# A planner that lays out a fused attention and gated-layer kernel: the first instruction of a tile becomes a condition of order alone for its other users

## Chip, cores and metric

One Trainium2 chip, one core of it. The kernel is written in Bass and Tile: it names the instructions of the engines itself, and the Tile layer adds the semaphores. The metric is the device time of one execution in microseconds (us). TensorE is called PE, VectorE DVE, ScalarE ACT, GpSimd POOL, and SyncE, whose queue issues most transfers, SP.

## The reference

A local attention (chunks of 32 queries, up to 64 keys with 8 of memory, 4 x 8 heads, 768 tokens, head dimension 64) feeds two gated layers on 3072 tokens with 512 features.

```python
scores = scale * np.matmul(q_c, k_full.transpose(0, 1, 3, 2))
a = np.exp(scores - max); a = a / (sum + 1e-9); out = a @ v_full
...
gate = 1.0 / (1.0 + np.exp(-(x @ w_gate)))          # 512 -> 1536
x = (gate * (x @ w_val)) @ w_out                     # 1536 -> 512
...
h = x @ w_in                                         # 512 -> 2048
P = a[0] + a[1]*h + a[2]*h**2 + a[3]*h**3
Q = 1.0 + abs(b[0])*abs(h) + abs(b[1])*h**2
y = (P / (Q + 1e-06)) @ w_out2                       # 2048 -> 512
```

Inputs and result are float32; the weights come as 64-bit words and are turned into float32 on the chip.

## The kernel before

**Work.** Every float32 operand of a large matrix product is split into a high part (an ACT copy to the reduced format) and the rest (a DVE subtraction), and three products of parts replace one. The tokens are cut into six blocks of 512 (index j). In the first layer, for block j and feature group f (12 of them), PE makes `h{j}_{f}_0` (gate) and `h{j}_{f}_1` (value), 12 matmuls of 512 columns each; ACT takes the sigmoid of the first into a tile called `sg{j}_{f}` (or, where two tiles share a buffer, by the name of the other half, as `wfo2` or `wfo7`); DVE multiplies; ACT and DVE split the product into `g1_{j}_{f}`; and 12 matmuls add it to `acc{j}`. The weights of group f come in three loads, `st1_{f}_0` to `st1_{f}_2`. For f = 1 and 2 the three loads share two buffers: `stp1_0` holds 1_1_0 and 1_1_1, `stp1_1` holds 1_1_2, and `stp2_0`, `stp2_1` likewise. `conv_scale` makes two ACT operations of 512 columns on each load, `conv_bits` one DVE operation that merges them (into `wfgv` or `wfo`), and then `wp1_{j}_{f}_{u}` is split off it, high part on ACT, rest on DVE.

**Start.** The attention of the first four groups of 128 tokens stands at the head of the program. For group t: `sp` (scores, PE), maximum, exponential and sums (DVE, ACT), a DVE multiplication `s<-s,r`, `tp` (four transposes, PE), an ACT copy `at<-tp`, `xp` (64 short products, PE), and the split of `x` (ACT copy `x<-xp`, DVE rest). Filler matmuls (`idle<-ones`) stand between them on PE. Then the first layer begins with `h0_0_0`.

**What sets the order.** Nothing is issued directly. A `Recorder` notes every call as a `Task` with the tiles that it touches. Its `plan()` runs the tasks through a model with costs of its own and hands out, engine by engine, the ready task with the earliest due time (`late`); `emit()` then issues them in that order. PE's order is fixed as written, so the planner only sets the order of ACT, DVE, POOL and SP around it. A task becomes a candidate when all tasks in its `deps` have been placed (`missing` is 0), and not before the time at which their results are there (`ready`). Due times run backwards over the same dependencies. In `access()` the first task that touches a tile of a pool (`c.first`) takes the buffer, and each other user of that tile gets it as a dependency:

```python
elif c.first is not t:
    t.deps.add(c.first)
```

So the second transfer into a half of `stp1_0` waited in the plan for the landing of the first, though the two halves are apart. Dependencies through the data itself are found further down in the same function, by overlapping regions. Buffers of PSUM are the `ps` pool (4 banks, shared by `sp`, `tp`, `xp` and `h`) and `acc`.

On the chip each engine works through its list in order and waits at the head for semaphores. All calls go through line 471 in the trace (line 480 with the change); tiles tell them apart.

Of the kernel before, what the change touches and what calls it, by code (L numbers as in the profile page):

```python
# [53 lines left out]
class Cell:  # L54


    def __init__(self, pool, make, dt, real=None):
        self.pool, self.make, self.dt, self.real = pool, make, dt, real
        self.accesses, self.users, self.first, self.group, self.left = [], set(), None, None, 0
# [115 lines left out]
class Task:  # L175
    def __init__(self, eng):
        self.eng, self.calls, self.deps, self.cells, self.gets = eng, [], set(), set(), []
        self.dur, self.lat, self.bytes, self.start, self.table, self.mark = 0.0, 0.15, 0, None, None, None
        self.window, self.cap, self.soon, self.late, self.fixed = 30.0, None, 0.0, 0.0, False
        self.ordered = True  # L180
# [10 lines left out]
class Recorder:  # L191
# [77 lines left out]
    def access(self, t, x, write):  # L269
        c, box = x.cell, x.box()  # L270
        if c.pool is not None and t not in c.users:
            if c.first is None:
                c.first = t
                t.gets.append(c)
            elif c.first is not t:
                t.deps.add(c.first)
            c.users.add(t)
            t.cells.add(c)
        keep = []
        for b, u, w in c.accesses:  # L280
            if b[0] < box[1] and box[0] < b[1] and b[2] < box[3] and box[2] < b[3]:
                if u is not t and (write or w):
                    t.deps.add(u)
                inside = box[0] <= b[0] and b[1] <= box[1] and box[2] <= b[2] and b[3] <= box[3]
                if write and inside or u is t and w == write and inside:
                    continue
            keep.append((b, u, w))
        keep.append((box, t, write))
        c.accesses = keep
# [24 lines left out]
    def plan(self):  # L314
        tasks = self.tasks
        for t in tasks:
            t.succ = []
        for t in tasks:
            t.missing, t.soft = len(t.deps), []
            for d in t.deps:  # L320
                d.succ.append(t)
            t.ready = 0.0
# [6 lines left out]
        for t in reversed(tasks):  # L329
            t.succ, t.hard = t.succ + t.soft, t.succ  # L330
            if t.eng == "tensor":
                t.late = min([t.soon] + [u.late - t.lat * (u.eng != "tensor") - t.dur for u in t.succ])
                continue
            lat = t.lat + (4.5 if t.bytes else 0)
            cap = t.cap if t.cap is not None else self.DMA_CAP if t.bytes else self.CAP
            t.late = min([t.soon + cap] + [u.late - lat - t.dur for u in t.succ])
        free = dict(self.sizes)
        cells = {c for t in tasks for c in t.cells}
        for c in cells:
# [14 lines left out]
        ready = {e: [t for t in tasks if t.eng == e and not t.missing] for e in engines}  # L354
        busy, dma, table = dict.fromkeys(engines, 0.0), 0.0, None
        order, ends, half, now, stall, left = [], [], None, 0.0, 0.0, len(tasks)
        events = []
        self.stalls = []
        while left:
            while ends and ends[0][0] <= now + 1e-9:  # L360
                free[heapq.heappop(ends)[1]] += 1
            moved = False
            for e in engines:
                if busy[e] > now + 1e-9:
                    continue
                head = fixed.get(e)
                if e == "tensor":
                    pick = pe[pe_i : pe_i + 1]
                elif head:
                    pick = head[:1]  # L370
                else:
                    pick = ready[e]
                best = None
                for t in pick:
                    if t.missing or t.ready > now + 1e-9 or best and best.late <= t.late:
                        continue
                    if not t.fixed and e != "tensor":
                        if t.late > now - stall + t.window:
                            continue
                        if t.bytes and dma > now + 7 and t.late > now - stall + 9:  # L380
                            continue
                    need, h = {}, half
                    for c in t.gets:
                        if c.pool == ("t", "half"):
                            if h:
                                h = None
                                continue
                            h = True
                        need[c.pool] = need.get(c.pool, 0) + 1
                    if all(  # L390
                        free[self.real_pool(p)] >= n + 2 * (n == 3) + (0 if t.fixed or p[0] not in (self.ORDERED if t.ordered else "g") else bisect_left(waiting[p], t.key))
                        for p, n in need.items()
                    ):
                        best = t
                if best is None:
                    continue
                t = best
                if e == "tensor":
                    pe_i += 1
                    if now - t.soon > stall + 0.05:  # L400
                        self.stalls.append((now, now - t.soon - stall, t))
                    stall = max(stall, now - t.soon)
                elif head:
                    head.pop(0)
                if e != "tensor":
                    ready[e].remove(t)
                extra = 0.0
                if t.table and t.table != table:
                    table, extra = t.table, 1.29
                t.start = now  # L410
                busy[e] = now + t.dur + extra
                end = now + t.dur + extra + t.lat
                if t.bytes:
                    dma = max(dma, now + 0.8) + t.bytes / self.RATE
                    end = dma + t.lat
                for c in t.gets:
                    waiting[c.pool].remove(t.key)
                    if c.pool == ("t", "half"):
                        if half:
                            c.group, half = half, None  # L420
                            c.group[0] = 2
                            continue
                        half = c.group = [1, 0, 0.0]
                    else:
                        c.group = [1, 0, 0.0]
                    free[self.real_pool(c.pool)] -= 1
                for c in t.cells:
                    c.left -= 1
                    g = c.group
                    g[2] = max(g[2], end)  # L430
                    if c.left == 0:
                        g[1] += 1
                        if g[1] == 2 or g[1] == g[0] and g is not half:
                            heapq.heappush(ends, (g[2], self.real_pool(c.pool)))
                for u in t.hard:
                    u.missing -= 1
                    u.ready = max(u.ready, end if u.eng != e or e != "tensor" else now + t.dur)
                    if not u.missing and u.eng != "tensor":
                        ready[u.eng].append(u)
                    heapq.heappush(events, u.ready)  # L440
                heapq.heappush(events, busy[e])
                order.append(t)
                left -= 1
                moved = True
            if not moved:
                while events and events[0] <= now + 1e-9:
                    heapq.heappop(events)
                nxt = events[0] if events else None
                if ends and (nxt is None or ends[0][0] < nxt):
                    nxt = ends[0][0]  # L450
                for e in engines[1:]:
                    for t in ready[e]:
                        w = t.late + stall - t.window
                        if now + 1e-9 < w and (nxt is None or w < nxt):
                            nxt = w
                if dma > now + 7:
                    nxt = dma - 7 + 1e-3 if nxt is None else min(nxt, dma - 7 + 1e-3)
                assert nxt is not None, (now, free, left, pe[pe_i].calls[0], [(e, len(ready[e])) for e in engines])
                now = max(nxt, now + 1e-6)
# [1606 lines left out]
```

## Time and profile before

| | us |
|---|---|
| median of 3 runs (lowest, highest) | 1134.45 (1133.39, 1134.48) |
| the profiled execution | 1134.46 |
| its span, first to last instruction | 1132.6 |
| PE busy | 1120.2 |
| DVE busy | 872.8 |
| ACT busy | 750.1 |

The 1.86 us between the profiled execution's time and its span lie outside the instructions. A busy PE is not PE at its peak, since matmuls are pipelined and their modelled ends overlap; what counts below are the times at which PE waits, and from one matmul's start to the next (2.72 us for 12 of 512 columns).

### The profile page before, as it was taken

To read this page: it belongs to the slowest core of one execution; us is meant where nothing else is said; L and a number is where in the kernel's file an instruction comes from. 1 tells how busy PE (TensorE), PEld (TensorE's weight loads), DVE (VectorE), ACT (ScalarE), POOL (GpSimd) and SP (SyncE) were. 2 spreads that over 40 slices of the span, in tenths; PEclk is the share of its full clock that TensorE was granted. 3 is DMA by queue.
4 is the path that set the end of the run, shared out by engine and by line. 5 is a ranking of instruction groups with operands and counts; after the bars stand their busy time and mean duration, and the time that the engine had idled before them with its cause. 6 is when DMAs were issued, how large, how long until landed. Compare 5 with 4: busy or idle time off the path is not lost.

```text
span 1132.6 us, 20033 instructions
## 1 busy us (share of the span) xinstructions
PE 1120.2 (99%) x7815; PEld 918.5 (81%) x7815; DVE 872.8 (77%) x1184; ACT 750.1 (66%) x1105; POOL 23.1 (2%) x39
## 2 busy tenths in 40 slices
PE   8999999999999999999999999999999999999998
PEld 4787888888888888888888788888888888888887
DVE  5788867774676667565568499999899999789984
ACT  4999556663454466343345599875799974898852
POOL 0000000000000000000000000000000000000000
PEclk8999999999999999999999999999999999999999
DMA  9899699997978799898976576689677788576764
GB/s 371 311 352 360 227 347 363 350 365 259 379 279 324 288 376 387 310 373 291 322 259 246 191 230 220 208 246 342 203 229 225 223 288 307 167 242 219 230 207 143
DMA packets 100318, 318.78 MB, mean 281 GB/s; under 512 B 10752, under 2 KB 11008, under 8 KB 100224
## 3 DMA queue, kind: packets, MB, share of 16 engines
q1 hardware_dynamic: 96192, 303.51, 74.3%
q0 software_dynamic: 3456, 12.58, 6.0%
q8 instruction: 62, 1.02, 0.4%
q10 hardware_dynamic: 576, 1.41, 0.3%
q14 instruction: 32, 0.26, 0.1%
HBM read 240.91 MB, written 63.96 MB: 269 GB/s over the span
## 4 chain that ended last, share of the span: by engine, by line
PE 96%; ACT 1%; DMA 1%; DVE 1%; issue 0%; DVEq 0%
PE acc L471 40%; PE p L471 20%; PE q_X L471 12%; PE h L471 10%; PE q_Z L471 6%; PE q_Y L471 3%; PE xp L471 2%; PE sp L471 1%; PE tp L471 1%; PE idle L471 1%; DMA st<-w_in 0%; DMA k<-k_in 0%; ACT L471 0%; ACT stp L471 0%; DVE s L471 0%
## 5 line engine op out<-in xcount | busy, mean ns | idle before, releaser
L471 PE MATMUL acc<-w2o,G 128*128 128x512 f32 x1152 | 268.4, 389 | 0.0
L471 PEld LDWEIGHTS acc<-w2o,G 128*128 128x128 f32 x1152 | 216.2, 188 | 44.9
L471 PE MATMUL acc<-g,wp 128*128 128x512 f32 x720 | 177.0, 393 | 0.0
L471 PEld LDWEIGHTS acc<-g,wp 128*128 128x128 f32 x720 | 133.3, 188 | 28.3 <-issue 0.2
L471 PE MATMUL q_X<-x,wi 128*128 128x512 f32 x576 | 146.5, 390 | 1.4 <-ACT hb L471 1.4
L471 PE MATMUL h<-x,wp 128*128 128x512 f32 x576 | 138.1, 392 | 1.7 <-ACT sg L471 0.9
L471 PE MATMUL p<-b,wpq_s 128*128 128x512 f32 x576 | 138.4, 389 | 0.0
L471 PEld LDWEIGHTS q_X<-x,wi 128*128 128x128 f32 x576 | 107.9, 188 | 24.7 <-ACT hb L471 2.5
L471 PEld LDWEIGHTS h<-x,wp 128*128 128x128 f32 x576 | 107.2, 188 | 25.0 <-ACT wp L471 1.1
L471 PEld LDWEIGHTS p<-b,wpq_s 128*128 128x128 f32 x576 | 108.1, 188 | 22.5
L471 ACT ACTIVATE st<-st 128x512 f32<-128x512 f32 (+1 forms) x124 | 76.7, 666 | 0.0
L471 PE MATMUL p<-x,wpq_a 128*128 128x512 f32 x288 | 73.2, 389 | 0.0
L471 PE MATMUL q_Z<-x,wi 128*128 128x512 f32 x288 | 73.1, 389 | 0.0
L471 ACT ACTIVATE u<-q,qc 128x1024 f32<-128x1024 f32 x48 | 54.9, 1147 | 14.4 <-DMA q<-u 13.2
L471 PEld LDWEIGHTS p<-x,wpq_a 128*128 128x128 f32 x288 | 54.0, 188 | 11.3
L471 PEld LDWEIGHTS q_Z<-x,wi 128*128 128x128 f32 x288 | 54.1, 188 | 11.2
L471 DVE SCALAR_TENSOR_TENSOR t<-t,cf,u 128x1024 f32<-128x1024 f32 x48 | 61.2, 1278 | 0.0
L471 DVE SCALAR_TENSOR_TENSOR q<-q,u 128x1024 f32<-128x1024 f32 x48 | 58.3, 1219 | 2.2 <-ACT u L471 2.1
L471 ACT ACTIVATE hb<-q_X 128x512 f32<-128x512 f32 x48 | 28.4, 592 | 36.4 <-PE q_X L471 36.3
L471 ACT ACTIVATE u<-u 128x1024 f32<-128x1024 f32 x48 | 50.3, 1055 | 0.4
L471 ACT ACT_TABLE_LOAD x31 | 39.8, 1283 | 15.8 <-PE h L471 7.2
L471 ACT ACTIVATE g<-c 128x512 fp32r<-128x512 f32 x22 | 13.8, 629 | 51.1 <-DVE c L471 51.1
(271 smaller groups left out, 1708.8 us busy)
## 6 DMA issues: line engine op xcount, KB each, us to landing
w2o<-w2o SPq DMA_DIRECT2D x96, 512.0 KB, 4.4
wi<-wq SPq DMA_DIRECT2D x72, 512.0 KB, 4.6
st<-w_in SPq DMA_DIRECT2D x62, 512.0 KB, 7.0
wp<-wqa SPq DMA_DIRECT2D x55, 512.0 KB, 6.6
wpq_s<-wqs SPq DMA_DIRECT2D x48, 512.0 KB, 8.1
wpq_a<-wqa SPq DMA_DIRECT2D x36, 512.0 KB, 7.6
wqa<-wp SPq DMA_DIRECT2D x30, 512.0 KB, 7.5
v<-v_in SPq DMA_DIRECT2D x24, 512.0 KB, 6.4
```

What stands on the lines that cost most here:

```text
L471: getattr(getattr(self.nc, t.eng), op)(*[real(x) for x in args], **{n: real(x) for n, x in kw.items()})
```

## The change

A new set `after` stands beside `deps`. The first task of a tile goes there for the other users of it, unless it is a true dependency as well. In the plan such a user may not be placed before the first task has been placed (it still counts in `missing`), but from then on it may go at once: its `ready` time is the moment of placing, not the end of the first task's work. In the due times the first task need only be as early as its user, with no duration or latency taken off.

```diff
 class Task:
     def __init__(self, eng):
         self.eng, self.calls, self.deps, self.cells, self.gets = eng, [], set(), set(), []
+        self.after = set()
...
             elif c.first is not t:
-                t.deps.add(c.first)
+                t.after.add(c.first)
...
         for t in tasks:
-            t.succ = []
+            t.succ, t.next = [], []
         for t in tasks:
-            t.missing, t.soft = len(t.deps), []
+            t.after -= t.deps
+            t.missing, t.soft = len(t.deps) + len(t.after), []
+            for d in t.after:
+                d.next.append(t)
...
-                t.late = min([t.soon] + [u.late - t.lat * (u.eng != "tensor") - t.dur for u in t.succ])
+                t.late = min([t.soon] + [u.late for u in t.next] + [u.late - t.lat * (u.eng != "tensor") - t.dur for u in t.succ])
...
-            t.late = min([t.soon + cap] + [u.late - lat - t.dur for u in t.succ])
+            t.late = min([t.soon + cap] + [u.late for u in t.next] + [u.late - lat - t.dur for u in t.succ])
...
+                for u in t.next:
+                    u.missing -= 1
+                    u.ready = max(u.ready, now)
+                    if not u.missing and u.eng != "tensor":
+                        ready[u.eng].append(u)
```

PE's list stays as it was. On SP the loads of the first weights change places; on ACT and DVE rows move mainly within blocks 0 and 1, and a few later. Three places follow. At the start, DVE's list before, from the multiplication of group 2 on (`s2<-s2,r2`; `r3` belongs to group 3, `x0_0` and `x0_1` are the first x tiles):

```order
L471 TENSOR_TENSOR s2_290<-s2_290,r2_343 128x512
L471 RECIPROCAL r3_355<-r3_355 128x8
L471 SCALAR_TENSOR_TENSOR wfgv0_410<-st1_0_0_135 128x512
L471 TENSOR_TENSOR s2_290<-s2_290,r3_355 128x512
L471 TENSOR_TENSOR x0_0_403<-xp0_0_363,x0_0_403 128x2x128
L471 TENSOR_TENSOR x0_1_412<-xp0_1_365,x0_1_412 128x2x128
L471 TENSOR_TENSOR wp1_0_0_0_418<-wfgv0_410,wp1_0_0_0_418 128x512
L471 SCALAR_TENSOR_TENSOR wfgv0_410<-stp1_0_133 128x512
```

The same stretch of DVE's list with the change:

```order
L480 SCALAR_TENSOR_TENSOR wfgv0_400<-st1_0_0_133 128x512
L480 TENSOR_TENSOR s2_292<-s2_292,r2_345 128x512
L480 RECIPROCAL r3_356<-r3_356 128x8
L480 TENSOR_TENSOR x0_0_402<-xp0_0_363,x0_0_402 128x2x128
L480 TENSOR_TENSOR s2_292<-s2_292,r3_356 128x512
L480 TENSOR_TENSOR x0_1_404<-xp0_1_365,x0_1_404 128x2x128
L480 TENSOR_TENSOR wp1_0_0_0_407<-wfgv0_400,wp1_0_0_0_407 128x512
L480 SCALAR_TENSOR_TENSOR wfgv0_400<-st1_0_1_139 128x512
```

The merge of the first weights now stands ahead of the two multiplications, and the multiplication of group 3 (by `r3`) now stands behind `x0_0`, which reads the products of group 0.

ACT's list before, from the conversion of the first weights to the table load for the first sigmoid, without the rows that read `xp` (those stand between):

```order
L471 ACTIVATE st1_0_0_135<-st1_0_0_135 128x512
L471 ACTIVATE stp1_0_133<-stp1_0_133 128x512
L471 ACTIVATE st1_0_0_135<-st1_0_0_135 128x512
L471 ACTIVATE at0_348<-tp1_357 128x512
...
L471 ACTIVATE stp2_1_231<-stp2_1_231 128x512
L471 ACTIVATE stp1_0_133<-stp1_0_133 128x512
L471 ACTIVATE stp2_0_139<-stp2_0_139 128x512
L471 ACT_TABLE_LOAD
L471 ACTIVATE wfo2_618<-h0_0_0_580 128x512
L471 ACTIVATE wp1_0_1_1_640<-wfgv0_410 128x512
```

The same two pieces of ACT's list with the change:

```order
L480 ACTIVATE st1_0_0_133<-st1_0_0_133 128x512
L480 ACTIVATE at0_349<-tp1_358 128x512
L480 ACTIVATE x0_0_402<-xp0_0_363 128x2x128
...
L480 ACTIVATE wp1_0_1_0_571<-wfgv0_400 128x512
L480 ACTIVATE st1_0_2_183<-st1_0_2_183 128x512
L480 ACTIVATE wp1_0_1_1_588<-wfgv0_400 128x512
...
L480 ACTIVATE stp2_0_230<-stp2_0_230 128x512
L480 ACT_TABLE_LOAD
L480 ACTIVATE sg0_0_627<-h0_0_0_580 128x512
```

Ahead of the copy of `tp1` one conversion operation is left of three, and `wp1_0_1_1`, the second weight tile of group f = 1, now stands eight rows ahead of the table load instead of two behind it.

The third place is on ACT around the sigmoid of `h0_7_0`, before:

```order
L471 ACTIVATE s6_1131<-s6_1131 128x512
L471 ACTIVATE wp1_0_9_0_1311<-wfgv4_1140 128x512
L471 ACTIVATE wp1_0_9_1_1349<-wfgv4_1140 128x512
L471 ACT_TABLE_LOAD
L471 ACTIVATE sg0_7_1356<-h0_7_0_1287 128x512
```

and with the change:

```order
L480 ACTIVATE s6_1127<-s6_1127 128x512
L480 ACT_TABLE_LOAD
L480 ACTIVATE sg0_7_1350<-h0_7_0_1283 128x512
L480 ACTIVATE x1_0_1357<-xp4_0_1310 128x2x128
L480 ACTIVATE x1_1_1366<-xp4_1_1312 128x2x128
L480 ACTIVATE sg0_7_1350<-tp5_1345 128x512
L480 ACTIVATE wp1_0_9_0_1371<-wfgv4_1154 128x512
L480 ACTIVATE wp1_0_9_1_1379<-wfgv4_1154 128x512
```

The two weight splits for f = 9 moved behind the sigmoid of f = 7; nothing else ahead of that sigmoid was added or taken away, only moved.

## Rows read from the trace of the kernel before

**Rows 1.** The page, part 1: busy us (share) xinstructions of each engine.

```profile
PE 1120.2 (99%) x7815; PEld 918.5 (81%) x7815; DVE 872.8 (77%) x1184; ACT 750.1 (66%) x1105; POOL 23.1 (2%) x39
```

**Rows 2.** Waits of PE, whole span: waiter, releaser, us in total, times, longest.

```profile
PE tp L471 <- DVE s L471: 3.1, 2, 1.6
...
PE q_X L471 <- ACT hb L471: 1.4, 2, 0.7
PE h L471 <- ACT sg L471: 0.9, 1, 0.9
PE h L471 <- ACT wp L471: 0.7, 1, 0.7
```

**Rows 3.** Windows: us, busy (x) of PE, PEld, DVE, ACT, POOL; clock, DMA.

```profile
40.00:95.00 55.00, 54.98 (x543) 44.31 (x542) 46.55 (x83) 54.83 (x95) 0.34 (x2) 1.00 0.94 340
125.00:260.00 135.00, 135.00 (x1518) 111.77 (x1511) 94.70 (x149) 82.26 (x138) 0.34 (x2) 1.00 0.94 344
```

**Rows 4.** Timeline of PE, 18 to 45 us: start, us, operation, count, idle before.

```profile
18.09 1.09 PE L471 MATMUL tp<-ident,s 128*128 128x128 f32 x4 [1.54 <-DVE s L471]
19.11 1.93 PE L471 MATMUL xp<-at,v 64*64 64x32 f32 x64
20.97 1.97 PE L471 MATMUL tp<-ident,s 128*128 128x128 f32 x8
22.73 1.49 PE L471 MATMUL idle<-ones 128*128 128x512 bf16 x3
24.14 1.24 PE L471 MATMUL xp<-at,v 64*64 64x32 f32 x64
...
26.07 1.14 PE L471 MATMUL xp<-at,v 64*64 64x32 f32 x64
...
27.89 1.14 PE L471 MATMUL xp<-at,v 64*64 64x32 f32 x64
...
29.86 7.19 PE L471 MATMUL h<-x,wp 128*128 128x512 f32 x30
37.76 4.73 PE L471 MATMUL h<-x,wp 128*128 128x512 f32 x18 [0.71 <-ACT wp L471]
42.33 2.88 PE L471 MATMUL acc<-g,wp 128*128 128x512 f32 x12
```

**Rows 5.** Timeline of DVE, 17 to 22 us.

```profile
17.25 0.69 DVE L471 TENSOR_TENSOR s<-s,r 128x512 f32<-128x512 f32 x1
...
20.08 0.68 DVE L471 TENSOR_TENSOR s<-s,r 128x512 f32<-128x512 f32 x1
21.50 0.76 DVE L471 TENSOR_TENSOR x<-xp,x 128x256 fp32r<-128x256 f32 x2 [0.74 <-ACT x L471]
```

**Rows 6.** Timeline of ACT, 19 to 37 us.

```profile
19.35 0.57 ACT L471 ACTIVATE at<-tp 128x512 f32<-128x512 f32 x1
21.09 0.66 ACT L471 ACTIVATE x<-xp 128x256 fp32r<-128x256 f32 x2 [1.17 <-PE xp L471]
...
31.78 3.50 ACT L471 ACTIVATE stp<-stp 128x512 int32<-128x512 uint32 x6
35.30 1.28 ACT L471 ACT_TABLE_LOAD   x1
```

**Rows 7.** Timeline of ACT, 92 to 97 us.

```profile
92.77 1.13 ACT L471 ACTIVATE wp<-wfgv 128x512 fp32r<-128x512 f32 x2
93.92 1.28 ACT L471 ACT_TABLE_LOAD   x1
95.21 0.60 ACT L471 ACTIVATE sg<-h 128x512 f32<-128x512 f32 x1
```

**Rows 8.** Timeline of PE, 92 to 97 us.

```profile
95.86 1.43 PE L471 MATMUL h<-x,wp 128*128 128x512 f32 x5 [0.88 <-ACT sg L471]
```

**Rows 9.** Windows of the start, columns as in rows 3; the clock stands before DMA.

```profile
18.00:24.00 6.00, 5.91 (x79) 4.52 (x79) 4.26 (x11) 4.46 (x10) 0.00 (x0) 0.50 1.03 404
...
26.00:30.00 4.00, 4.00 (x138) 2.84 (x137) 3.08 (x7) 3.91 (x10) 0.00 (x0) 1.00 1.02 407
```

## Prediction

> **What bounds the kernel now.** I read the page first: PE is busy for 1120.2 of 1132.6 us [rows 1], and its list is the same with the change. So time can be won only where PE waits for another engine, and lost only where a new wait arises. The list of PE's waits comes next [rows 2]. Apart from the first transfers there are four: 3.1 us for the softmax multiplication `s` on DVE (two waits, ahead of the transposes), 0.7 us for a weight split `wp` on ACT, 0.9 us for a sigmoid `sg` on ACT, and 1.4 us for `hb` copies in the second layer, where neither ACT's nor DVE's nor SP's list changes. The windows say who is short where [rows 3]: from 40 to 95 us ACT is busy for 54.83 of 55.00 us, so everything that ACT does late at the start is still late at 95 us. From 125 to 260 us it is busy for only 82.26 of 135; there and later PE has no wait until `hb`, and the few rows that move there move by one or two places. I take the change to be decided in the first 96 us.
>
> **The change part by part.**
>
> *Group 3's transposes come later.* Before, DVE multiplies group 3 at 20.08 [rows 5] and PE runs the transposes of groups 2 and 3 in one piece, 20.97 to 22.94 [rows 4], group 3's from about the middle, 21.9. With the change that multiplication stands behind `x0_0`, which can't start before 21.50, since it waits for ACT's copy of `xp0`, and PE's `xp0` is not moved by the change. Two x rows in 0.76 us with a duration of about 0.4 give a step of 0.34, so the multiplication runs from 21.85 and ends 0.69 later, at 22.54. From the end of the other `s<-s,r` (17.25 + 0.69) to the transposes that waited for it (18.09) is 0.15: PE starts at 22.69, **0.8 us later**. Fillers, `xp1` to `xp3` and the first `h` follow without a wait before, so all of them move by as much: `h` from 29.86 to 30.7.
>
> *The weights of group f = 1 come earlier.* The first 30 `h` matmuls run from 29.86; at 0.227 each (2.72 for 12) the 48 up to `acc` would take 10.9 us, to 40.75. `acc` starts at 42.33, 1.6 later. About 0.2 of that is at the very start, for the first x parts, and stays. The rest, **1.36**, is the wait for `wp1_0_1_1` at 37.76 (0.71 of it idle, the remainder the pipeline's own and the wait for the tile's DVE half). In the new list this tile's ACT half stands eight rows ahead of the table load (8 x 0.56, so before 32 us) and its DVE half follows; PE needs it at 37.7. The wait goes. `acc` then starts at 42.33 + 0.82 - 1.36 = **41.8, 0.54 earlier**.
>
> *ACT falls behind.* This is the term that I think decides. One conversion costs a step of 0.56 (six in 3.50 us, the last one 0.68) [rows 6], a weight split 0.52 (1.13 for two, 0.1 of it a tail) [rows 7], a pair of x copies 0.55 (0.66 with its tail) and a copy `at` 0.5 (0.57 with its tail) [rows 6]. Before, ACT fills the time up to the copy of `tp1` with three conversions; in the new list one is left, and the two that went don't come until PE has been waited for. I follow the new list: the copy of `tp1` at 19.22 (the transposes end at 18.09 + 1.09), `xp0` at 21.09 as before; x pair, split, conversion, `at2`, two conversions, `at3`, split, done at 25.36; `xp1` ends at 24.14 + 1.24 + 0.82 = 26.20; x pair, two conversions, 27.93; `xp2` ends at 28.03; x pair, one conversion, 29.18; `xp3` ends at 29.85; then x pair, three splits and seven conversions (0.55 + 1.56 + 3.92, and 0.16 for the last one's tail), and the table load starts at 36.1 instead of 35.30 [rows 6], 0.8 later, with one conversion fewer done. **ACT is 0.8 + 0.56 = 1.36 us behind** with everything that follows.
>
> *The sigmoid of f = 7 comes earlier in ACT's list.* Between 40 and 95 us ACT has nothing to catch up with. The sigmoid that PE waits for at 95.86 [rows 8] ends at 95.81 [rows 7]. The two splits that moved behind it take 2 x 0.52 off: 95.81 - 1.04 + 1.36 = 96.13, and PE starts at 96.18, **0.33 later than before**. PE itself would be there at 95.86 - 0.88 - 0.54 = 94.4, so 1.75 us of new waits between 42 and 95 us would be free. What PE wins at 37.76 it gives back here.
>
> *The rest at nothing.* The loads keep their number, and the first of the weights takes the same place in SP's list, with another tile. Table loads keep their number as well. The splits for f = 9 are needed at about 110 us and now come some 2 us later than before; ACT has a gap after 115 us to end its backlog in. If that cover were gone, each would cost 0.52.
>
> *Sum.* Against the profiled execution (1134.46 us, 0.01 over the median of the three runs): +0.33, so **1134.8 us**. The bounds: if the sigmoid does not hold PE up at all, -1.42 (0.88 + 0.54); if the 0.82 of the transposes is doubled for ACT by a slower start, +1.2.
>
> **Rivals.** *1. The clock stays low for longer.* [...] PE had been working without a wait since 18.09 when it rose. The new wait of some 0.6 us lies inside that stretch. It came back between 24 and 26, some 6.7 us after 18.09. If it comes back as long after 22.69, at 29.4, `xp1`, a filler and most of `xp2` run at the low level. `xp` takes 1.93 there against 1.14 [rows 4], 1.7 times; over the 2.7 us of work in question this is +1.7, and ACT passes it on in full, since it waits for each `xp`: 1136.5. If the clock stays low until `h`, the 4.9 us from `xp1` to the end of `xp3` become 8.1: +3.3, so 1138.1, and **slower**. The point from which it is slower by over 0.2% (2.27 us, about what a measurement of this kernel tells from no change) is a clock that comes back later than about 30 us. For it: the fall came after waits like this one. Against: the new wait is less than half as long as each of the two that brought the clock down, and fillers follow it. [...]
>
> *2. ACT is not behind at 95 us.* If DVE's new order lets ACT's work come so that the idle steps are made up, or the sigmoid is early for another reason, PE passes at up to 94.4 instead of 95.86: 1133.0 to 1134.2. For it: two more splits are out of the way, and PE is early. Against: ACT has no idle time to give from 40 to 95 us [rows 3].
>
> *3. Little moves.* The change reorders mainly blocks 0 and 1, and what is won and lost may cancel to 1134.5 without the gate deciding; this can't be told from my forecast by the time, only by the rows.
>
> *4. A new wait elsewhere* after 96 us, from a row that lost its place on ACT or DVE (the x combinations near 230 and 430 us, the splits near 690). Each such place would cost about one operation, 0.5 to 0.7 us; it would take four of them for 0.2%.
>
> **How the numbers follow.** My forecast (1134.2 to 1135.6): 0.63. Rival 1: 0.18 with the clock back by 30 us (up to 1136.8), 0.07 later than that. Rival 2: 0.07. Rival 4: 0.05, of which 0.02 beyond 0.2%. The likeliest time is 1134.8; from 1133.2 to 1136.7 holds some 0.85 to 0.9, the forecast, most of rival 2 and the first half of rival 1. No case that I can price wins more than 1.42 us, less than 0.2%, so faster gets 0.03, for what I have not seen; slower gets 0.07 and 0.02 and a little for the unseen, 0.10; the rest, 0.87, is within 0.2%.
>
> **What would show it.** Right: a wait of PE for `s` ahead of the second set of four transposes, near 22.1 to 22.7; `h` from about 30.7; no wait for `wp` near 38; `acc` near 41.8; the first table load of the sigmoid on ACT near 36.1; and a wait of PE for `sg` near 96, some 1.7 us long instead of 0.88, ended at about 96.2. Wrong: that wait gone or shorter than 0.9 (ACT was not behind), windows with a clock of 0.50 beyond 26 us, or a PE wait of over 0.5 us at a place that isn't named here. It goes wrong most easily through the clock, or through ACT waiting for DVE somewhere between 40 and 95 us, where each microsecond is one of the kernel.

## The result, and the profile after

The changed kernel takes 1142.31 us (median of six executions), the kernel before 1134.30 (six beside them): a ratio of 1.0057, with a 95% interval of 1.0033 to 1.0080. It is slower by 0.57%. The six lie in two groups: 1136.72 and 1137.15, and four from 1142.21 to 1142.54. The prediction was 1134.8, with a range that ended at 1136.7.

The profiled execution is the fastest one, of 1136.72 us (span 1134.7). Its list of PE's waits answers to [rows 2]:

```profile
PE tp L480 <- DVE s L480: 3.7, 3, 1.6
PE h L480 <- ACT sg L480: 1.9, 1, 1.9
```

There is a third wait for `s`, the wait for `sg` is twice as long, and the one for `wp` is gone. The timeline of PE, beside [rows 4] and [rows 8]:

```profile
20.92 1.11 PE L480 MATMUL tp<-ident,s 128*128 128x128 f32 x4
22.62 1.09 PE L480 MATMUL tp<-ident,s 128*128 128x128 f32 x4 [0.59 <-DVE s L480]
23.50 1.34 PE L480 MATMUL idle<-ones 128*128 128x512 bf16 x3
24.77 1.14 PE L480 MATMUL xp<-at,v 64*64 64x32 f32 x64
...
30.38 11.28 PE L480 MATMUL h<-x,wp 128*128 128x512 f32 x48
41.49 2.88 PE L480 MATMUL acc<-g,wp 128*128 128x512 f32 x12
...
96.06 4.60 PE L480 MATMUL h<-x,wp 128*128 128x512 f32 x12 [1.91 <-ACT sg L480]
100.50 2.88 PE L480 MATMUL acc<-g,wp 128*128 128x512 f32 x12
```

The timeline of ACT, beside [rows 6, 7]:

```profile
35.78 1.28 ACT L480 ACT_TABLE_LOAD   x1
...
95.41 0.60 ACT L480 ACTIVATE sg<-h 128x512 f32<-128x512 f32 x1
```

Every row that was forecast stands within 0.4 us of its place, and the wait at the gate of f = 7 ends at 96.06 for a forecast of 96.18. But behind that wait 12 matmuls take 4.60 us from first to last. In the kernel before, the same rows are:

```profile
95.86 3.02 PE L471 MATMUL h<-x,wp 128*128 128x512 f32 x12 [0.88 <-ACT sg L471]
98.72 2.88 PE L471 MATMUL acc<-g,wp 128*128 128x512 f32 x12
```

The windows of the changed kernel say why (the clock stands before the DMA share, as in [rows 9]):

```profile
18.00:24.00 6.00, 5.37 (x78) 4.29 (x79) 4.14 (x11) 3.85 (x9) 0.00 (x0) 0.50 1.03 404
24.00:26.00 2.00, 2.00 (x68) 1.22 (x67) 1.14 (x2) 1.40 (x4) 0.00 (x0) 0.86 0.99 391
...
95.00:100.00 5.00, 3.94 (x10) 3.12 (x11) 2.97 (x7) 4.99 (x11) 0.00 (x0) 0.66 1.03 398
```

After the wait of 1.91 us, PE's clock was at 0.50 of full speed from 97 to 99 us (0.62 in the microsecond before, 0.67 in the one after); the mean of 95 to 100 us is 0.66. In the kernel before it is 1.00 there. So in this execution PE is 0.20 us late when it leaves the wait (96.06 for 95.86), and 1.8 us late at the next `acc` (100.50 for 98.72 before). This explains most of the lower group. The upper group needed a trace of its own, which two later executions of the same kernel gave (1142.61 and 1141.76 us). Timeline of PE in the first of these:

```profile
22.77 1.09 PE L480 MATMUL tp<-ident,s 128*128 128x128 f32 x4 [0.59 <-DVE s L480]
23.65 1.49 PE L480 MATMUL idle<-ones 128*128 128x512 bf16 x3
25.07 1.93 PE L480 MATMUL xp<-at,v 64*64 64x32 f32 x64
...
35.21 11.10 PE L480 MATMUL h<-x,wp 128*128 128x512 f32 x42
...
102.08 4.60 PE L480 MATMUL h<-x,wp 128*128 128x512 f32 x12 [1.92 <-ACT sg L480]
106.52 2.90 PE L480 MATMUL acc<-g,wp 128*128 128x512 f32 x12
```

and its windows:

```profile
24.00:26.00 2.00, 2.00 (x39) 1.09 (x40) 1.12 (x2) 1.52 (x3) 0.00 (x0) 0.50 1.00 397
26.00:30.00 4.00, 4.00 (x107) 2.83 (x101) 1.69 (x4) 1.77 (x4) 0.00 (x0) 0.50 1.02 407
30.00:38.00 8.00, 8.00 (x91) 5.06 (x87) 4.19 (x8) 5.64 (x13) 0.00 (x0) 0.52 0.59 230
38.00:50.00 12.00, 12.00 (x55) 9.91 (x53) 8.19 (x14) 11.65 (x21) 0.00 (x0) 1.00 0.70 233
```

The matmuls and these two waits are the same (0.59 at 22.77, 1.92 at 102.08). But the clock stays at 0.50 from 18 to 30 us, and the mean of 30 to 38 is 0.52, where the execution of 1136.72 has it back before 26 (0.86 in 24 to 26, 1.00 in 26 to 30). The first `h` starts at 35.21 for 30.38, and the gate of f = 7 is passed at 102.08 for 96.06: 6.0 us, about what lies between the groups. Of the nine executions of the changed kernel, six are of the upper group; the 75 of the kernel before that were timed beside all runs lie between 1133.39 and 1135.57.

### The profile page after: what moved, and what is told of

It reads as the page before. It is cut to its first block, busy times and chain, and to the rows that moved or that the text cites. A ratio compares the mean times of both kernels' runs of the same rounds, so it can differ in the third digit from the quotient of the medians.

```text
span 1134.7 us, 20035 instructions
## 1 busy us (share of the span) xinstructions
PE 1121.4 (99%) x7815; PEld 919.6 (81%) x7815; DVE 873.4 (77%) x1184; ACT 751.3 (66%) x1105; POOL 23.1 (2%) x39
## 3 DMA queue, kind: packets, MB, share of 16 engines
q8 instruction: 62, 1.02, 0.3%
q10 hardware_dynamic: 576, 1.41, 0.3%
## 4 chain that ended last, share of the span: by engine, by line
PE 91%; ACT 2%; issue 0%; DVE 0%
PE acc L480 39%; PE p L480 20%; PE q_X L480 12%; PE h L480 8%; PE q_Z L480 6%; PE q_Y L480 3%; PE xp L480 2%; PE sp L480 1%; PE tp L480 1%; ACT st L480 1%; ACT wp L480 0%; ACT L480 0%; ACT hb L480 0%; ACT s L480 0%; ACT g L480 0%
```

## The experiments

Three theories stood after the first profile. **1:** the wait at 96 us brings the clock down, for a longer or a shorter time, and this makes both groups. **2:** the new wait of 0.6 us at the start (group 3's transposes) keeps the clock down for longer, in some executions. **3:** the second loss lies behind 125 us. In the edits, `order` is the list that the planner returns, just before it is issued; `at(engine, written, read)` finds a task in it, and `move(task, ahead_of)` changes its place.

**The changed kernel once more**, for the place of the second loss.

> The changed kernel as it is, for another profile: six executions gave 1136.7, 1137.2 and four times 1142.2 to 1142.5. [...] Theory 2 (the new wait of 0.6 us ahead of group 3's transposes holds the clock down at the start): a profile of about 1142 shows a clock of 0.50 beyond 25 us, h later than 31, and ACT later by as much. [...] If it comes out at 1137 again, it shows the same two shifts as before, +0.2 at 96.06 and +1.6 by 100 us.

1137.5 us, so of the lower group, with the same two waits, and so nothing new of the upper group. It has one wait more: 0.76 us for "issue" (nothing that the profile shows) among the `xp` products at 28.25. The mean clock of the whole execution is 0.995, as in the one of 1136.72, so no long stretch at 0.50 came with this wait, and the first `h` starts 1.07 us later than in the execution of 1136.72 (31.45 for 30.38). The executions of one group thus differ at the start as well.

**The wait at 96 us filled.** PE makes group 5's transposes six times instead of once, and works while the sigmoid is on its way.

```diff
+        order[at("tensor", "tp5")].calls *= 6
```

> The changed kernel, where PE makes the four transposes of tp5, the last work ahead of the wait for the sigmoid of f = 7, six times instead of once (same result each time), so that PE works through most of its 1.9 us of waiting. The order on all engines stays. Theory 1: the clock stays at full speed at 96 us, h0_7_1 starts at 96.1 as before, and the 1.6 us lost behind it and whatever makes 1142 are gone: 1135.1 (1134.7 to 1135.4) in all executions. Theory 2 or 3: the executions still fall into about 1137 and about 1142.

1137.75, 1142.44, 1142.50 and 1142.56 us. The profiled one is of the upper group. Its PE timeline and windows:

```profile
99.17 2.84 PE L503 MATMUL tp<-ident,s 128*128 128x128 f32 x24
101.76 3.00 PE L503 MATMUL h<-x,wp 128*128 128x512 f32 x12
104.59 2.88 PE L503 MATMUL acc<-g,wp 128*128 128x512 f32 x12
...
441.63 0.32 PE L503 MATMUL xp<-at,v 64*64 64x32 f32 x8 [2.02 <-issue]
```

```profile
30.00:38.00 8.00, 7.35 (x78) 5.08 (x81) 4.38 (x9) 5.92 (x13) 0.00 (x0) 0.54 0.57 222
...
95.00:100.00 5.00, 5.00 (x86) 4.14 (x86) 4.42 (x9) 4.95 (x9) 0.00 (x0) 1.00 0.97 301
```

No wait for `sg` is left, the clock doesn't fall there (1.00 in 97 to 105 us), and the 12 `h` take 3.00 instead of 4.60 us. The upper group stays all the same, with the low clock up to 38 us. Theory 1 as the cause of two groups falls, and theory 3 has its answer too: the clock is low up to 38 us here as in the execution of 1142.61 (0.54 in 30 to 38 us, for 0.52), where that had cost 6.0 us by the gate. By the next `acc` this execution is 1.93 us ahead of that one (104.59 for 106.52), 1.6 of it by the filling and 0.3 from ahead of the gate. It was lost again at 441 us, in a wait of 2.02 us for "issue" (see the end).

**The wait at 95 us of the kernel before made longer.** A weight split of ACT ahead of the sigmoid is made three times.

```diff
+        order[at("scalar", "wp1_0_9_1")].calls *= 3
```

> The kernel before, with the ACT split of wp1_0_9_1, which stands ahead of the sigmoid of f = 7, made three times instead of once (same result), 2 x 0.52 more of ACT's work: the wait at 95.86 grows from 0.88 to 1.9 us. Nothing else of the change is in it. Theory 1: 1.04 for the wait, and 1.6 for the clock that falls then: 1137.0 (1136.7 to 1137.4), with some executions near 1142. Theory 2 or 3: 1135.4, the wait alone.

Median 1135.67 (ratio 1.0018, 1.0008 to 1.0027). Of ten executions seven lie from 1135.22 to 1135.80, the others at 1137.13, 1138.75 and 1138.88. The last one is profiled:

```profile
97.45 5.49 PE L494 MATMUL h<-x,wp 128*128 128x512 f32 x12 [2.23 <-ACT sg L494]
```

```profile
97.00:105.00 8.00, 7.55 (x20) 5.96 (x21) 3.04 (x7) 6.00 (x13) 0.00 (x0) 0.58 0.79 278
```

With a wait of 2.23 us, 1.35 longer than in [rows 8], the clock falls (0.58 in 97 to 105 us), and 12 matmuls take 5.49 us. This execution also has a wait of 1.41 us for "issue" at 26.65, with a second low stretch behind it (28.8 to 32 us; the mean is 0.82 in 26 to 30 and 0.88 in 30 to 38); by the gate that leaves some 0.3 us. Most executions are longer by only about the wait itself. That those are without the fall at the gate is argued from their time alone, since none has a trace. But a trace shows a wait about this long without a fall: behind the 2.02 us at 441 us in the variant before, the clock stayed at 1.00 (the row is at the end).

**The wait at 96 us taken away.** In the changed kernel the exponential of group 6 on ACT, with its sums and multiplication on DVE, is moved behind the sigmoid of f = 7 and the x copies, which also saves two table loads.

```diff
+        late = [at("scalar", "s6", "", 2), *[at("vector", "r6", "", n) for n in range(3)], at("vector", "s6", "", 1)]
+        late = [order[i] for i in late]
+        for t in late:
+            order.remove(t)
+        n = max(at("scalar", "at5", "tp5"), at("vector", "x1_1", "xp4_1")) + 1
+        order[n:n] = late
```

> The changed kernel, with the exponential of group 6 and the DVE operations on its sum moved behind the sigmoid of f = 7 and the x copies after it, so that two table loads fall away and the sigmoid follows h0_7_0 at once: no wait at 96. Theory 1: PE goes through at 94.2, 1.9 us for the wait and 1.6 for the clock come off 1136.7: 1133.2 (1132.8 to 1133.8), in all executions; faster than the kernel before by about 1.1 us. Theory 2: the executions still differ by 5 us among themselves, 1133 and 1138. Theory 3: as theory 2.

Ten executions: six from 1132.80 to 1133.91, four from 1138.36 to 1139.01 (ratio of all 1.0009, 0.9993 to 1.0024). PE passes the gate without a wait, at 94.79 in the profiled one. The lower group falls by some 3.7 us, and the upper one with it: the two losses add up, and taking one away leaves the other.

**Group 3's multiplication put back** ahead of the first x addition, in the changed kernel:

```diff
+        move(("vector", "s3", "r3"), ("vector", "x0_0", "xp0_0"))
```

> The changed kernel, with group 3's normalizing multiply put back ahead of the first x addition on VectorE, as in the kernel before; all else as changed. TensorE's transposes of group 3 should then start without their wait of 0.6 us. [...] Theory 1 (the two values come from the wait at 96 us): still about two of three executions near 1142. Theory 3 (they come from behind 125 us): the same as theory 1.

Eleven executions from 1135.18 to 1137.57, median 1135.86 (ratio 1.0014, 1.0006 to 1.0023); the upper group is gone, as theory 2 has it. PE's timeline and the window in which the clock comes back:

```profile
20.64 1.97 PE L503 MATMUL tp<-ident,s 128*128 128x128 f32 x8
...
94.94 4.60 PE L503 MATMUL h<-x,wp 128*128 128x512 f32 x12 [1.89 <-ACT sg L503]
...
404.69 2.89 PE L503 MATMUL acc<-g,wp 128*128 128x512 f32 x12
```

```profile
24.00:26.00 2.00, 2.00 (x95) 1.42 (x90) 1.14 (x3) 2.00 (x6) 0.00 (x0) 1.00 1.03 406
```

**The same multiplication put behind, in the kernel before**, and nothing else of the change:

```diff
+        t = order.pop(at("vector", "s3", "r3"))
+        order.insert(at("vector", "x0_0", "xp0_0") + 1, t)
```

> The kernel before, with only group 3's normalizing multiply on VectorE moved behind the first x addition, as the change has it. The wait of 0.6 us of group 3's transposes should come to be, the one at 96 us stays 0.9 us. Theory 2: two values, 1134.5 to 1135.5 and about 5.3 us more (1140), the longer ones with the clock low until 38 us and a mean granted clock of about 0.991. Theories 1 and 3: one value, 1134.3 to 1135.

Ten executions: four from 1134.30 to 1135.68, six from 1138.44 to 1139.87. This row alone makes the upper group. PE and the clock in the profiled one (1138.59):

```profile
22.31 1.09 PE L495 MATMUL tp<-ident,s 128*128 128x128 f32 x4 [0.59 <-DVE s L495]
...
24.61 1.93 PE L495 MATMUL xp<-at,v 64*64 64x32 f32 x64
```

```profile
26.00:30.00 4.00, 4.00 (x89) 2.62 (x85) 1.45 (x3) 1.87 (x5) 0.00 (x0) 0.50 1.02 408
30.00:38.00 8.00, 8.00 (x85) 5.29 (x84) 4.80 (x9) 6.51 (x14) 0.00 (x0) 0.68 0.30 115
```

The clock comes back earlier here than in the execution of 1142.61 (0.68 in 30 to 38 us, for 0.52), and the group lies some 4 us over the lower one where 5.3 were expected.

**The wait at the start filled**, in the changed kernel: PE makes group 2's transposes twice, and DVE's order stays as changed. This tells the idleness of PE from the order of the rows around it.

```diff
+        order[at("tensor", "tp2")].calls *= 2
```

> The changed kernel, in which TensorE makes group 2's transposes twice over (the same result written again, some 1.1 us), so that it works through the 0.6 us for which it waited for group 3's multiply; VectorE's order stays as changed. If it is TensorE's idleness that keeps the clock low (theory 2): no execution near 1142, all at 1137 to 1138. If it is the order of the work around it, and not the idle 0.6 us, or theories 1 and 3: about two of three executions near 1142 to 1143.

Twelve executions: eleven from 1134.98 to 1138.19, one of 1141.47 (median 1137.05, ratio 1.0023, 1.0013 to 1.0032). The profiled one (1136.80):

```profile
20.52 2.82 PE L503 MATMUL tp<-ident,s 128*128 128x128 f32 x12
```

```profile
24.00:26.00 2.00, 2.00 (x72) 1.31 (x75) 1.13 (x3) 1.94 (x6) 0.00 (x0) 1.00 1.01 401
```

It is the idle time of PE, not the order of DVE's rows: with PE busy through the 0.6 us, the clock is back by 24 us (1.00 in 24 to 26 us, for 0.50 in the execution of 1142.61). One execution in twelve is still long, and five lie at 1135 to 1136, lower than expected; neither kind has a trace, so why stays open.

**The wait at 96 us filled, without the one at the start:** group 3's multiplication put back, and group 5's transposes made five times.

```diff
+        move(("vector", "s3", "r3"), ("vector", "x0_0", "xp0_0"))
+        order[at("tensor", "tp5")].calls *= 5
```

> [...] The hidden units behind the sigmoid should start where they did. [...] If the low clock costs nothing of its own there: 1135.5 to 1136.2, or longer by what the filling delays.

1135.72 to 1139.72, median 1138.10 (ratio 1.0029, 1.0017 to 1.0040): in its time a miss, as the 1.6 us of the low clock taken off would have made it 1134.0 to 1134.6. Its trace still has the answer:

```profile
92.71 2.40 PE L504 MATMUL tp<-ident,s 128*128 128x128 f32 x20
95.27 3.06 PE L504 MATMUL h<-x,wp 128*128 128x512 f32 x12 [0.15 <-ACT sg L504]
...
403.45 2.89 PE L504 MATMUL acc<-g,wp 128*128 128x512 f32 x12
...
436.32 0.30 PE L504 MATMUL xp<-at,v 64*64 64x32 f32 x4 [1.95 <-issue]
```

The 12 `h` leave the gate at full clock (1.00 in 95 to 100 us) and take 3.06 us. At 403 us this kernel is 1.24 us ahead of the one with the multiplication alone put back (403.45 for 404.69), though it left the gate 0.33 later: 1.57 us for the clock, as the 4.60 less 3.02 say. Behind 404 us it lost more than that: 1.1 in a wait for ACT at 409 us, 1.95 at 436 us in a wait for issue, and a low clock behind this one (0.83 in 430 to 440 us).

**Both moves together:** group 3's multiplication ahead, and group 6's exponential behind the sigmoid.

```diff
+        move(("vector", "s3", "r3"), ("vector", "x0_0", "xp0_0"))
+        late = [at("scalar", "s6", "", 2), *[at("vector", "r6", "", n) for n in range(3)], at("vector", "s6", "", 1)]
...
+        order[n:n] = late
```

> The changed kernel with two moves: group 3's multiply ahead of the first x addition (no wait at 22 us), and the exponential and the normalizing of group 6 behind the sigmoid of f=7 (no wait at 96 us, two table loads of ScalarE fewer). Theory 2 with the wait at 96 us as a second, separate loss: one value, 1132.5 to 1134, in all executions, at or below the kernel before. If the second value has another source: part of the executions near 1138.5.

Eleven executions from 1131.32 to 1133.87, median 1131.92: a ratio of 0.9978 to the kernel before (0.9969 to 0.9987). It beats both kernels, and has one group. The gate of f = 7 and the window behind it:

```profile
92.10 0.66 PE L509 MATMUL tp<-ident,s 128*128 128x128 f32 x4
92.51 3.02 PE L509 MATMUL h<-x,wp 128*128 128x512 f32 x12
```

```profile
95.00:100.00 5.00, 5.00 (x24) 4.14 (x23) 4.43 (x9) 4.50 (x9) 0.00 (x0) 1.00 1.03 410
```

**The exponential behind the sigmoid, in the kernel before**, with nothing of the change:

```diff
+        late = [at("scalar", "s6", "", 2), *[at("vector", "r6", "", n) for n in range(3)], at("vector", "s6", "", 1)]
...
+        order[n:n] = late
```

> The kernel before, with the exponential and the normalizing of group 6 moved behind the sigmoid of f=7 (no wait of 0.9 us at 95 us, two table loads of ScalarE fewer), and nothing of the change. If the gain of the version with both moves comes from this move and not from the change: 1131.5 to 1133.5, like that version (1131.92). If the change gives part of it: 1133.5 to 1134.3.

1132.47 to 1134.60, median 1133.57 (0.9991, 0.9982 to 1.0000). PE at the gate:

```profile
94.34 3.02 PE L499 MATMUL h<-x,wp 128*128 128x512 f32 x12
```

The version with both moves is lower by 1.65 us, so the change itself is worth something once its two waits are gone: PE starts the `h` of the gate at 92.51 there, and at 94.34 here. Most of this is the wait for `wp` that the change removes: from the first `h` to the first `acc` it is 11.11 us there (28.88 to 39.99) and 12.46 here (29.36 to 41.82).

**Two more executions of the changed kernel**, for a trace of the upper group; the first is shown above.

> The changed kernel as it is, one look, to have its own trace of an execution near 1142 (four of its six were). [...] Near 1137: the clock low for 6.8 us at the start, and the trace tells nothing new.

> The changed kernel as it is, a second look of the same kind: near 1142 with the clock low from about 17 to 38 us, or near 1137 with 6.8 us of it (theory 2).

1142.61 and 1141.76 us. In the second too the clock is low up to 38 us (0.54 in 26 to 38 us), with the waits of 0.59 and 1.96.

## Why the prediction was wrong

*Group 3's transposes come later*: right in the lower group. They start at 22.62 (22.69 forecast) after a wait of 0.59, and `h` at 30.38 (30.7): of the 0.8 us, 0.3 were won back before `h`, because the clock was up again ahead of `xp1` (1.14 us for 1.24).

*The weights of group f = 1 come earlier*: right. No wait for `wp` is left, the 48 matmuls run in one piece, and `acc` starts at 41.49 (41.8).

*ACT falls behind* and *The sigmoid of f = 7 comes earlier in ACT's list*: right. The table load starts at 35.78 (36.1), and the gate costs 1.91 us (1.75) and opens at 96.06 (96.18). The sum of +0.33 measured +0.20 at this place, in the lower group.

**The step that failed is the weighing of rival 1**, *The clock stays low for longer*, and with it the sum, which has the length of each wait and not what the clock does behind it. Two things were wrong.

The first is the weight of "Against: the new wait is less than half as long as each of the two that brought the clock down, and fillers follow it". That holds, and didn't help: the 0.59 us inside the low stretch were enough to keep the clock at 0.50 up to some 38 us in six of nine executions (two of the six have a trace, the others are counted by their time). Put alone into the kernel before, the row that makes this wait gives the upper group in six of ten; put back, none of eleven. The rival had a chance of 0.25 and a price of at most +3.3 (its own 8.1 less 4.9 are 3.2), with a clock that is back by the first `h`. In the execution of 1142.61 the clock came back later still, when `h` had been running for over 2 us, and the price measured is 6.0. The rival's middle case, a return some 6.7 us behind the new wait, at 29.4, was met in no trace of a kernel with this wait: the clock was back before 26 us in three of them (two have 1.00 in 26 to 30 us, the third has the same mean of 0.995 over the whole as the execution of 1136.72) and at 35 to 38 us in four (0.50 in 26 to 30 us in three, 0.54 over 26 to 38 in the other). (Its price of +1.7 is 1.9 by its own factor: 2.7 us at 1.7 times.) One program thus took different times: the traces of 1136.72 and 1142.61 have the same rows up to 23 us (the wait of 0.59 ends at 22.62 and 22.77), and the clock back before 26 us or at 38. What decides between the two was not shown. The 5.9 us between them are 0.52% of 1136.7. They are yet three quarters of the 8.0 us by which the medians differ.

The second is that the wait at the gate was taken as a wait and no more. The profile had what was needed: waits of 1.54 and 1.6 us for `s` [rows 2, 4] stand ahead of the stretch at 0.50 [rows 9], and the 0.88 at 95.86 left the clock alone (1.00 in 95 to 100 us). A wait of 1.75 us was forecast, longer than the ones that stood before the low clock; the fall behind it should have been a term of the sum. It was put at nothing, and measured 1.6 us (4.60 less 3.02, which 12 matmuls take at this place in the trace of before), confirmed from the other side by the filled gate (1.57). In all six traces with a wait of 1.9 to 2.0 us at this gate the 12 took 4.49 to 4.60; the mean clock is 0.66 in 95 to 100 us in three of them, and 0.83 in 100 to 110 us in the two of the upper group.

So: of the 2.26 us of the lower group, 0.2 are the wait as forecast, 1.6 are the clock behind it, and the other 0.5 come behind that `acc`: 0.28 in 30 `acc` matmuls at 435 us (7.36 us to the next row, for 7.08 before), and 0.16 outside the span (2.02 us lie there, for 1.86 before), both without a cause shown; the upper group's further 6 us are the clock at the start. "No case that I can price wins" held, and of the rivals 2, 3 and 4 nothing was seen beyond those 0.28 us.

## What to carry to other kernels

A wait of PE had two prices here, its length and the matmuls at a clock of 0.50 behind it, and the second was up to ten times the first: 0.6 us of waiting cost 6 us in six of nine executions, where it fell into a stretch in which the clock was still low. The second price was not paid every time (not in the other three, nor behind the 2.02 us at 441 us), so it belongs in the sum with a chance. Compare each new wait with the shortest one of the trace that has a low clock behind it, and look above all for waits inside a low stretch, as here at the start of the program. Where executions fall into groups, take a trace of each group before explaining the median, and mend both waits: here two moves turned +0.57% into -0.22%.

## What the runs showed of the hardware

In five variants PE waited for "issue", nothing that the profile shows, at one place of the program, near the end of the same 128 `xp` products or up to 12 matmuls behind them: 0.20 us at 435.89 (exponential behind the sigmoid), 0.50 at 437.84 (group 3's multiplication put back), 1.05 at 437.87 (filled start), 1.95 at 436.32 and 2.02 at 441.63 (filled gate). The windows of the variant with the gate filled and no wait at the start:

```profile
420.00:430.00 10.00, 10.00 (x164) 8.26 (x163) 8.68 (x16) 8.61 (x17) 0.00 (x0) 1.00 1.00 351
430.00:440.00 10.00, 8.05 (x151) 6.68 (x150) 4.94 (x9) 4.47 (x9) 0.00 (x0) 0.83 1.02 383
```

and of the filled gate with the wait at the start:

```profile
440.00:450.00 10.00, 8.37 (x48) 7.04 (x49) 4.74 (x8) 5.40 (x10) 0.00 (x0) 1.00 1.03 409
```

Behind the 1.95 us the clock falls (0.83 is the mean), behind the 2.02 us it stays at 1.00. So the length of a wait alone did not decide here whether the clock falls.

What PE waited for stays open. All 16 DMA engines are busy there (a share of 1.00 to 1.03), but they are so in the trace of before too, which has no such wait (1.04 and 1.02 from 420 to 440 us). The three variants with matmuls added to PE's list have the three longest waits, the other two have the list unchanged; no run tested why.
